# SSM tables: upper half of X left as two unsummed products, small Y levels built for 128 channels at once, seed copies on ScalarE

## The chip, the cores and the metric

The kernel runs on one core of one Trainium2 chip. The metric is device time in microseconds (us); lower is better. All traces shown here are of one execution on core 0. One run of the kernel before took 769 us against 607 for the others; such slow runs are left out of every comparison. "Fast" below means the undisturbed state.

## The reference, cut to what matters

Four layers: an SSM convolution, local attention, the same SSM convolution again, local attention again. Only the first SSM layer is touched. It builds, for each of 512 channels, a convolution kernel K of length 2048 from 128 complex modes, and applies it by FFT.

```python
def _A_ref(u, A_re, A_im, B_re, B_im, C_re, C_im, log_dt, Dskip):
    dt = jnp.exp(log_dt)[:, None]
    logdA = dt * (A_re + 1j * A_im)
    dB = dt * (B_re + 1j * B_im)
    P = jnp.exp(logdA[:, :, None] * l[None, None, :])      # 512 x 128 x 2048 powers
    K = jnp.einsum("dn,dnl,dn->dl", Cc, P, dB).real        # one kernel per channel
    ...                                                    # rfft of K and u, product, irfft
    return y + u * Dskip
```

## The kernel before

The 2048 powers are not computed one by one. A time step is split into a pair (e, i): X holds 32 powers, Y holds 64 scaled powers, and K[e, i] is the sum over the 128 modes of X[e] times Y[i], with real and imaginary parts. That sum is a matmul per channel, so TensorE does it, while VectorE has to build X and Y. The 512 channels come in eight "halves" of 64; two halves are one block of 128 channels, for which the FFT work is done.

Tables grow by doubling: a level of m entries becomes 2m entries by two products and one sum (a complex multiplication; `MA` and `MB` hold the multipliers, with the signs folded in). The top of Y is different: there the two products are kept apart in `Y` and `Y2` and *not* added, and TensorE adds them by accumulating one more matmul.

```python
    def double(self, T, m, lev, hc):
        for e0 in range(0, m, HALF):                 # HALF = 8: at most 1024 elements an operation
            ...
            nc.vector.tensor_tensor(v(ta), src, self.mult(self.MA, lev, hc, mm), ALU.mult)
            nc.vector.tensor_tensor(v(tb), src, self.mult(self.MB, lev, hc, mm), ALU.mult)
            nc.vector.tensor_tensor(T[... m + e0:m + e0 + mm ...], ta[...], tb[:, ::-1 ...], ALU.add)

    def x_part(self, X, hc):
        ...
        nc.vector.tensor_copy(X[:, :, :, 1, :]..., self.nu[:, hc]...)
        for lev in range(1, 5):
            self.double(X, 1 << lev, 6 + lev, hc)    # lev 4: 16 -> 32 entries, six operations

    def y_base(self, Y, hc):
        self.nc.vector.tensor_copy(Y[:, :, :, 0, :]..., self.cb[:, hc]...)
        for lev in range(4):
            self.double(Y, 1 << lev, lev, hc)

    def contract(self, X, Y, Y2, hc, half=None):
        ...
        for ds in range(n):                          # 16 channels of each column group
            for m in range(4):                       # real/imaginary, Y or Y2
                for g in range(4):                   # four groups of 32 columns of the array
                    ...
                    if m % 2 == 0:
                        nc.tensor.matmul(psk[32 * g:32 * g + 32, ds, :], xs, Y[...], ...)
                    else:
                        nc.tensor.matmul(psk[32 * g:32 * g + 32, ds, EYB:], xs, Y2[...], ...)
```

That is 256 matmuls per half, each preceded by its weight load: 512 TensorE instructions. The order of the work, cut:

```python
        xcs[0] = cv.u_fft(0)                         # FFT of the input, one block ahead
        for dc in range(4):
            Kt = half(dc * 2, (lambda: k_fft(dc - 1)) if dc > 0 else None)
            if dc > 0:
                cv.finish(dc - 1, xcs.pop(dc - 1), Kt, Xr)    # products pa, pb on VectorE, inverse FFT
            if dc < 3:
                def mid(dc=dc):
                    xcs[dc + 1] = cv.u_fft(dc + 1)
                half(dc * 2 + 1, mid)
        ...                                          # half 7 (of 0..7) in two parts, last block, layer 2
```

`half` builds the tables and then calls `contract` with high priority in the compiler's list scheduler. The tiles `Y`, `Y2` are single-buffered, `X` double.

## Time and profile before

| | kernel before |
|---|---|
| time (median of fast runs) | 607 us |
| span of the profiled run, granted TensorE clock | 606.0 us, 0.888 |
| first contraction starts | 61.7 us |
| last contraction ends | 226.9 us |
| from there to the end | 379.1 us |

The page of the whole run says that VectorE (DVE) is busy most, but a share over the whole span mixes stages:

```profile
span 606.0 us, 12631 instructions
PE 422.6 (70%) x5362; PEld 261.7 (43%) x5402; DVE 497.0 (82%) x942; ACT 323.0 (53%) x449; POOL 12.9 (2%) x50
```

The windows view of just the contraction loop decides it. The columns are the stretch, its length, the busy time and number of instructions of PE (matmul), PEld (weight load), DVE, ACT (ScalarE) and POOL, then the TensorE clock, the DMA share and GB/s:

```profile
core 0: us, PE busy (x) PEld busy (x) DVE busy (x) ACT busy (x) POOL busy (x), PEclk, DMA share, GB/s
61.67:226.90 165.23, 109.12 (x2653) 74.60 (x2664) 154.37 (x290) 79.15 (x94) 1.75 (x12) 0.81 0.48 95
```

VectorE works 154 of 165 us there: it bounds the loop.

Next, the VectorE timeline (start, length, engine, line, operation, output and input tiles, shapes). Table building begins at 38.9 us; the last three rows are part of the last doubling of X:

```profile
38.89 0.27 DVE L476 TENSOR_TENSOR ta<-Ytab,MA 128x128 bf16<-128x128 bf16 x1
...
55.30 1.23 DVE L513 TENSOR_TENSOR Ytab<-Ytab,MA 128x2048 bf16<-128x2048 bf16 x1
...
59.50 0.69 DVE L476 TENSOR_TENSOR ta<-Xtab,MA 128x1024 bf16<-128x1024 bf16 x1
60.11 0.68 DVE L477 TENSOR_TENSOR tb<-Xtab,MB 128x1024 bf16<-128x1024 bf16 x1
60.83 0.69 DVE L478 TENSOR_TENSOR Xtab<-ta,tb 128x1024 bf16<-128x1024 bf16 x1
```

The TensorE timeline of the first contraction shows matmuls in groups of four, and then a hole. The bracket gives the idle time and what ended it; "issue" means that the profile shows nothing the engine waited for:

```profile
61.67 0.25 PE L532 MATMUL psk<-Ytab,Xtab 128*32 128x64 bf16 x4 [3.00 <-DVE Xtab L478]
...
63.74 0.23 PE L535 MATMUL psk<-Y2tab,Xtab 128*32 128x48 bf16 x1
65.75 0.20 PE L535 MATMUL psk<-Y2tab,Xtab 128*32 128x48 bf16 x3 [1.78 <-issue]
```

From 61.67 to 63.74 us some 180 matmuls ran, about 12 ns each. Then came 1.78 us of nothing. Each contraction before, but for the last, which is split in two, has at least one such hole; from start to end one takes 4.7 to 10.6 us.

On ScalarE one group, the normalization of the input, ends at 61.1 us. And on TensorE, the last contraction is followed at once by the FFT of the last channels:

```profile
50.39 10.67 ACT L575 ACTIVATE X<-X,ln_nb_a,ln_rstd_a 128x512 bf16<-128x512 bf16 x15
```

```profile
226.64 0.22 PE L535 MATMUL psk<-Y2tab,Xtab 128*32 128x48 bf16 x4
226.79 0.20 PE L204 MATMUL psA<-KT,sb_F 128*128 128x64 bf16 x1
```

### The profile page before, as it was taken

How to read it: one execution, taken by the hardware profiler on the slowest of the kernel's cores; microseconds unless marked ns; L12 is line 12 of the kernel's file. 1: busy time of each engine (PE TensorE's matmuls, PEld its weight loads, DVE VectorE, ACT ScalarE, POOL GpSimd, SP SyncE). 2: the span in 40 equal slices, each digit the busy share in tenths (PEclk: the TensorE clock that was granted, in tenths of full speed). 3: DMA queues.
4: the chain of work that ended last, by engine and by line, in shares of the span. 5: the costliest groups of instructions: out<-in, count | busy, mean ns of one | idle time of the engine just before them, and what ended most of it. 6: DMA issues, size and time to landing. Idle time of an engine off the chain costs nothing.

```text
span 606.0 us, 12631 instructions
## 1 busy us (share of the span) xinstructions
PE 422.6 (70%) x5362; PEld 261.7 (43%) x5402; DVE 497.0 (82%) x942; ACT 323.0 (53%) x449; POOL 12.9 (2%) x50
## 2 busy tenths in 40 slices
PE   1102565865775575559998678977996899857996
PEld 0101343562462463245333466644764433326762
DVE  5999999799899996366877899965999688689950
ACT  4999355455465343526576213466984556722144
POOL 0000000000000002100000000000000000000000
PEclk9999787696797797758999599997998899978999
DMA  8101354624735627510001333005530000040011
GB/s 293 62 1 35 61 104 66 140 55 106 121 98 99 103 91 136 129 70 1 1 1 39 83 137 143 2 1 125 85 71 0 2 1 1 1 121 1 1 71 69
DMA packets 75093, 41.31 MB, mean 68 GB/s; under 512 B 65825, under 2 KB 70818, under 8 KB 73758
## 3 DMA queue, kind: packets, MB, share of 16 engines
q1 hardware_dynamic: 73454, 40.12, 27.2%
q8 instruction: 42, 0.69, 0.5%
q10 hardware_dynamic: 1584, 0.39, 0.3%
q14 instruction: 13, 0.11, 0.1%
HBM read 15.89 MB, written 8.39 MB: 40 GB/s over the span
## 4 chain that ended last, share of the span: by engine, by line
PE 27%; DVE 21%; ACT 9%; issue 7%; DMA 2%; POOL 0%; SPq 0%; POOLq 0%; ACTq 0%
PE ps_qk L822 7%; DVE prod L924 6%; PE ps_o L948 4%; PE ps_v L836 3%; PE Lp L868 2%; PE pt_x L802 2%; PE po L939 2%; DVE prod L863 1%; DVE ln_st_b L152 1%; ACT xc L711 1%; DVE pa L719 1%; DMA zt<-Z 1%; DVE pb L720 1%; ACT oT L942 1%; PE ps_o L950 1%
## 5 line engine op out<-in xcount | busy, mean ns | idle before, releaser
L939 PE MATMUL po<-sb_ident,prod 128*128 128x128 bf16 x1024 | 70.4, 227 | 13.7 <-DVE prod L924 10.3
L939 PEld LDWEIGHTS <-prod 128*128 128x128 bf16 x1024 | 62.3, 102 | 23.5 <-DVE prod L924 20.1
L822 PE MATMUL ps_qk<-xnT,wqk 128*128 128x512 bf16 x245 | 63.7, 391 | 4.3 <-ACT xnT L807 2.3
L855 DVE TENSOR_TENSOR prod<-qT,kT 128x2048 bf16<-128x2048 bf16 (+3 forms) x48 | 43.2, 953 | 14.0 <-ACT qT L824 7.2
L924 DVE TENSOR_TENSOR prod<-V,L 128x2048 bf16<-128x2048 bf16 (+3 forms) x48 | 43.8, 955 | 6.4 <-PE po L939 6.4
L942 ACT CAST oT<-po 128x1024 bf16<-128x1024 f32 x16 | 15.4, 1015 | 56.6 <-PE po L939 56.6
L863 DVE TENSOR_TENSOR prod<-qT,kT 128x2048 bf16<-128x2048 bf16 (+3 forms) x40 | 35.0, 903 | 6.9 <-ACT kT L824 4.3
L204 PE MATMUL psA<-X,sb_F 128*128 128x128 bf16 x128 | 13.7, 237 | 34.5 <-ACT X L575 33.7
L822 PEld LDWEIGHTS <-wqk 128*128 128x128 bf16 x256 | 23.4, 100 | 32.1 <-issue 11.8
L948 PE MATMUL ps_o<-wo_t,oT 128*128 128x512 bf16 x121 | 33.5, 380 | 4.9 <-ACT oT L942 3.9
L204 PEld LDWEIGHTS <-sb_F 128*128 128x128 bf16 x256 | 17.4, 106 | 42.6 <-issue 40.0
L924 DVE TENSOR_TENSOR prod<-Vp,L 128x2048 bf16<-128x2048 bf16 (+3 forms) x40 | 35.0, 903 | 0.0
L532 PE MATMUL psk<-Ytab,Xtab 128*32 128x64 bf16 x1024 | 23.7, 206 | 12.9 <-DVE Ytab L513 5.6
L191 ACT CAST Z<-psA 128x1024 bf16<-128x1024 f32 (+1 forms) x32 | 28.6, 979 | 7.3 <-PE psA L204 7.3
L535 PE MATMUL psk<-Y2tab,Xtab 128*32 128x48 bf16 x1024 | 22.8, 202 | 13.5 <-issue 12.2
L868 PE MATMUL Lp<-prod,sb_bones 128*32 128x512 bf16 x256 | 24.9, 410 | 10.1 <-DVE prod L863 5.1
L513 DVE TENSOR_TENSOR Ytab<-Ytab,MA 128x2048 bf16<-128x2048 bf16 (+1 forms) x33 | 30.7, 931 | 0.2
L152 DVE BATCH_NORM_STATS2 ln_st_b<-X 128x6 f32<-128x384 bf16 (+2 forms) x80 | 23.7, 358 | 8.6 <-ACT X L309 8.6
L515 DVE TENSOR_TENSOR Y2tab<-Ytab,MB 128x2048 bf16<-128x2048 bf16 (+1 forms) x33 | 30.7, 930 | 0.0
L836 PE MATMUL ps_v<-wv,xnT 128*128 128x512 bf16 x126 | 28.2, 379 | 1.8 <-ACT V L838 1.7
L532 PEld LDWEIGHTS <-Xtab 128*32 128x32 bf16 x1024 | 20.9, 105 | 17.8 <-issue 15.5
L222 PE MATMUL psA<-zt,sb_C 128*128 128x512 bf16 x30 | 15.6, 548 | 18.6 <-DMA zt<-Z 14.4
(184 smaller groups left out, 1022.3 us busy)
## 6 DMA issues: line engine op xcount, KB each, us to landing
kt_scratch<-Kt SPq DMA_DIRECT2D x4, 1024.0 KB, 3.9
Kt<-kt_scratch SPq DMA_DIRECT2D x4, 1024.0 KB, 6.8
Vp<-V SPq DMA_DIRECT2D x2, 1568.0 KB, 9.1
X<-in_A_u_dram SPq DMA_DIRECT2D x4, 512.0 KB, 5.1
Xr<-in_A_u_dram SPq DMA_DIRECT2D x4, 512.0 KB, 5.1
out_dram<-X SPq DMA_DIRECT2D x4, 512.0 KB, 2.6
k_scratch<-KTq SPq DMA_DIRECT2D x7, 256.0 KB, 2.0
KT<-k_scratch SPq DMA_DIRECT2D x7, 256.0 KB, 2.8
```

The lines of the kernel that those rows point to most:

```text
L204: nc.tensor.matmul(o, F1[:, j, r, :], rhs_j(j), start=True, stop=not dk)
L513: nc.vector.tensor_tensor(v(Y[:, :, :, q * EYB:(q + 1) * EYB, :]), src, vm(self.mult(self.MA, lev, hc, EYB)), ALU.mult)
L515: nc.vector.tensor_tensor(v(Y2[:, :, :, (q - 1) * EYB:q * EYB, :]), src, vm(self.mult(self.MB, lev, hc, EYB)), ALU.mult)
L532: nc.tensor.matmul(psk[32 * g:32 * g + 32, ds, :], xs, Y[:, m // 2, h, :, t], start=(m == 0), stop=False, skip_group_check=True)
L822: nc.tensor.matmul(ps[:], wqk[:, ct, f0:f0 + 128], xnT[:, ct, s0:s0 + 512], start=(ct == 0), stop=(ct == 3))
L836: nc.tensor.matmul(ps[:].rearrange("p a b -> p (a b)"), xnT[:, ct, j * 128:(j + 1) * 128], wv[:, ct, :], start=(ct == 0), stop=(ct == 3))
L855: nc.vector.tensor_tensor(pr[:, :, (ja - j0) * 128:(ja - j0) * 128 + n], qT[fp][:, :, ja * 128: ja * 128 + n], kT[fp][:, :, (ja - sh) * 12 ...
L863: nc.vector.tensor_tensor(pr[:, :, 0:n], qT[fp][:, :, q0: q0 + n], kT[fp][:, :, k0: k0 + n], ALU.mult)
L868: nc.tensor.matmul(Lp[r0:r0 + 32, w // 4, :], bones[:, w % 4, :], pr[:, f2, hb * 512:(hb + 1) * 512], start=(w % 4 == 0), stop=(w % 4 == 3 ...
L924: nc.vector.tensor_tensor(p2[:, ja - j0: ja - j0 + n, :].rearrange("p j (t d h) -> p (j t) d h", t=2, d=DH), src.rearrange("p j (t d h) -> ...
L939: nc.tensor.matmul(po[f2][:, jj, :], p2[:, jj, f2 * 128:(f2 + 1) * 128], ident[:], start=(w == 0 and jj % 4 == 0), stop=(w == W - 1), skip ...
L948: nc.tensor.matmul(ps[:], oT[:, ft, j * 128:(j + 1) * 128], wo_t[:, ft, :], start=(ft == 0), stop=False)
```

## The change

The intent is to take work off VectorE, which bounds the loop: (a) the last doubling of X becomes two products of 2048 elements, left unsummed, as was already done for Y; TensorE adds them with twice as many matmuls; (b) the small levels of Y are built for both halves of a block at once; (c) the three small copies that seed the tables move to ScalarE. To make room in memory, (d) the FFT of the input is done one step later with one buffer instead of two. The two halves of X now lie in swapped order, so (e) the results are fetched in two pieces that swap them back. Core of the diff, cuts marked with "...":

```diff
-        xc = self.one.tile([128, 4, 2, 512], BF, name="xc", tag="xc", bufs=2)
+        xc = self.one.tile([128, 4, 2, 512], BF, name="xc", tag="xc", bufs=1)
...
+    def y_seed(self, dc):
+        S = self.ty.tile([128, 2, 2, HD, HALF, 2], BF, name="Yseed", tag="Yseed")
+        self.nc.scalar.copy(S[:, :, :, :, 0, :]..., self.cb[:, dc * 2:dc * 2 + 2]...)
+        for lev in range(3):
+            m = 1 << lev
+            self.double(S[:, :, :, :, 0:m, :], S[:, :, :, :, m:2 * m, :], m, lev, dc * 2, dc * 2 + 2)
+        return S
+    def y_base(self, S, hc):
+        Y = self.ty.tile([128, 2, HD, EY, 2], BF, name="Ytab", tag="Ytab")
+        b = hc % 2
+        self.nc.scalar.copy(Y[:, :, :, 0:HALF, :]..., S[:, b]...)
+        self.double(S[:, b:b + 1], Y[:, :, :, HALF:2 * HALF, :].unsqueeze(1), HALF, 3, hc, hc + 1)
+        return Y
...
+    def x_products(self, X, hc):
+        X2 = self.ty.tile([128, 2, HD, EXB, 2], BF, name="X2tab", tag="X2tab")
+        src = X[:, :, :, EX - EXB:EX, :]...
+        for dst, M in ((X[:, :, :, 0:EXB, :], self.MA), (X2[:], self.MB)):
+            nc.vector.tensor_tensor(dst..., src, self.mult(M, 10, hc, hc + 1, EXB), ALU.mult)
+        return X2
...
-            for m in range(4):
+            for m in range(8):
+                c, low, summed = m // 4, m // 2 % 2, m % 2
                 for g in range(4):
...
+                    xs = X2[:, 1 - c, h, :, t] if low else X[:, c, h, :, t]
...
-        xcs[0] = cv.u_fft(0)
...
-                    xcs[dc + 1] = cv.u_fft(dc + 1)
+                    xcs[dc] = cv.u_fft(dc)
...
+        xcs[3] = cv.u_fft(3)
```

More of the change, by code (lines that the diff above doesn't have):

```diff
@@ L31 @@
 EX = 32
+EXB = 16
 EYB = 16
@@ L361, in tmp @@
     def tmp(name):
-        return pp.tile([128, 4, NM], F32, name=name, tag="ktmp", bufs=8)
+        return pp.tile([128, 4, NM], F32, name=name, tag="ktmp", bufs=6)
     tb = tmp("tb")
@@ L368, in ladder @@
     rnd = tmp("rnd")
-    ws = tmp("ws")
+    ws = rnd
     nc.vector.tensor_scalar(rnd[:], tb[:], MAGIC, MAGIC, ALU.add, ALU.subtract)
@@ L375, in ladder @@
     nc.scalar.activation(sn[:], ws[:], ACT.Sin, scale=TWO_PI)
-    cs = tmp("cs")
+    cs = sh
     nc.vector.tensor_tensor(cs[:], sh[:], sh[:], ALU.mult)
@@ L459, in __init__, with mult, double @@
         self.wk = es.enter_context(tc.tile_pool(name="t_w", bufs=1))
-    def mult(self, M, lev, hc, n):
-        return (M[:, lev, hc].rearrange("n c (h t) -> n (c h) t", t=2).unsqueeze(2)
-                .to_broadcast([128, 2 * HD, n, 2]))
-    def double(self, T, m, lev, hc):
+    def mult(self, M, lev, h0, h1, n):
+        return (M[:, lev, h0:h1].rearrange("n b c (h t) -> n (b c h) t", t=2).unsqueeze(2)
+                .to_broadcast([128, (h1 - h0) * 2 * HD, n, 2]))
+    def double(self, src, dst, m, lev, h0, h1):
@@ L467, in double @@
         nc = self.nc
-        for e0 in range(0, m, HALF):
-            mm = min(m, HALF)
-            ta = self.wk.tile([128, 2, HD, HALF * 2], BF, name="ta", tag="ta")
-            tb = self.wk.tile([128, 2, HD, HALF * 2], BF, name="tb", tag="tb")
-            def v(t):
-                return t[:].rearrange("n c h (e t) -> n (c h) e t", t=2)[:, :, 0:mm, :]
-            src = T[:, :, :, e0:e0 + mm, :].rearrange("n c h e t -> n (c h) e t")
-            nc.vector.tensor_tensor(v(ta), src, self.mult(self.MA, lev, hc, mm), ALU.mult)
-            nc.vector.tensor_tensor(v(tb), src, self.mult(self.MB, lev, hc, mm), ALU.mult)
-            nc.vector.tensor_tensor(T[:, :, :, m + e0:m + e0 + mm, :].rearrange("n c h e t -> n c h (e t)"),
-                                    ta[:, :, :, 0:mm * 2], tb[:, ::-1, :, 0:mm * 2], ALU.add)
@@ L481, in build @@
-    def build(self, hc):
+        nb = h1 - h0
+        n = nb * 2 * HD * m * 2
+        ta = self.wk.tile([128, 2 * HD * HALF * 2], BF, name="ta", tag="ta")
+        tb = self.wk.tile([128, 2 * HD * HALF * 2], BF, name="tb", tag="tb")
+        for t, M in ((ta, self.MA), (tb, self.MB)):
+            nc.vector.tensor_tensor(t[:, 0:n].rearrange("n (x e t) -> n x e t", e=m, t=2),
+                                    src.rearrange("n b c h e t -> n (b c h) e t"), self.mult(M, lev, h0, h1, m),
+                                    ALU.mult)
@@ new lines, in v @@
+        def v(t):
+            return t[:, 0:n].rearrange("n (b c h x) -> n b c h x", b=nb, c=2, h=HD)
+        for b in range(nb):
+            nc.vector.tensor_tensor(dst[:, b].rearrange("n c h e t -> n c h (e t)"), v(ta)[:, b], v(tb)[:, b, ::-1],
+                                    ALU.add)
+    def y_seed(self, dc):
+        S = self.ty.tile([128, 2, 2, HD, HALF, 2], BF, name="Yseed", tag="Yseed")
+        self.nc.scalar.copy(S[:, :, :, :, 0, :].rearrange("n b c h t -> n (b c h) t"),
+                            self.cb[:, dc * 2:dc * 2 + 2].rearrange("n b c (h t) -> n (b c h) t", t=2))
+        for lev in range(3):
+            m = 1 << lev
+            self.double(S[:, :, :, :, 0:m, :], S[:, :, :, :, m:2 * m, :], m, lev, dc * 2, dc * 2 + 2)
+        return S
@@ L482, in build, with x_base @@
+    def y_base(self, S, hc):
+        Y = self.ty.tile([128, 2, HD, EY, 2], BF, name="Ytab", tag="Ytab")
+        b = hc % 2
+        self.nc.scalar.copy(Y[:, :, :, 0:HALF, :].rearrange("n c h e t -> n (c h) (e t)"),
+                            S[:, b].rearrange("n c h e t -> n (c h) (e t)"))
+        self.double(S[:, b:b + 1], Y[:, :, :, HALF:2 * HALF, :].unsqueeze(1), HALF, 3, hc, hc + 1)
+        return Y
+    def x_base(self, hc):
         nc = self.nc
-        Y = self.ty.tile([128, 2, HD, EY, 2], BF, name="Ytab", tag="Ytab")
@@ L484, in build @@
-        Y2 = self.ty.tile([128, 2, HD, EY - EYB, 2], BF, name="Y2tab", tag="Y2tab")
         X = self.tx.tile([128, 2, HD, EX, 2], BF, name="Xtab", tag="Xtab")
-        return X, Y, Y2
-    def x_part(self, X, hc):
-        nc = self.nc
-        nc.gpsimd.memset(X[:, 0, :, 0, :], 1.0)
-        nc.gpsimd.memset(X[:, 1, :, 0, :], 0.0)
-        nc.vector.tensor_copy(X[:, :, :, 1, :].rearrange("n c h t -> n (c h) t"),
-                              self.nu[:, hc].rearrange("n c (h t) -> n (c h) t", t=2))
-        for lev in range(1, 5):
-            self.double(X, 1 << lev, 6 + lev, hc)
@@ L497, in y_base @@
-    def y_base(self, Y, hc):
-        self.nc.vector.tensor_copy(Y[:, :, :, 0, :].rearrange("n c h t -> n (c h) t"),
-                                   self.cb[:, hc].rearrange("n c (h t) -> n (c h) t", t=2))
-        for lev in range(4):
-            self.double(Y, 1 << lev, lev, hc)
-    def y_products(self, Y, Y2, hc, h0=0, h1=HD):
+        B = X[:, :, :, EX - EXB:EX, :]
+        nc.gpsimd.memset(B[:, 0, :, 0, :], 1.0)
+        nc.gpsimd.memset(B[:, 1, :, 0, :], 0.0)
+        nc.scalar.copy(B[:, :, :, 1, :].rearrange("n c h t -> n (c h) t"),
+                       self.nu[:, hc].rearrange("n c (h t) -> n (c h) t", t=2))
@@ new lines, in x_base @@
+        B = B.unsqueeze(1)
+        for lev in range(1, 4):
+            m = 1 << lev
+            self.double(B[:, :, :, :, 0:m, :], B[:, :, :, :, m:2 * m, :], m, 6 + lev, hc, hc + 1)
+        return X
+    def x_products(self, X, hc):
+        nc = self.nc
+        X2 = self.ty.tile([128, 2, HD, EXB, 2], BF, name="X2tab", tag="X2tab")
+        src = X[:, :, :, EX - EXB:EX, :].rearrange("n c h e t -> n (c h) e t")
+        for dst, M in ((X[:, :, :, 0:EXB, :], self.MA), (X2[:], self.MB)):
+            nc.vector.tensor_tensor(dst.rearrange("n c h e t -> n (c h) e t"), src,
+                                    self.mult(M, 10, hc, hc + 1, EXB), ALU.mult)
+        return X2
@@ L505, in y_products @@
+    def y_products(self, Y, hc, h0=0, h1=HD):
         nc = self.nc
+        if h0 == 0:
+            self.Y2 = self.ty.tile([128, 2, HD, EY - EYB, 2], BF, name="Y2tab", tag="Y2tab")
+        Y2 = self.Y2
         if h1 - h0 == HD:
@@ L513, in y_products, with contract @@
                 nc.vector.tensor_tensor(v(Y[:, :, :, q * EYB:(q + 1) * EYB, :]), src,
-                                        vm(self.mult(self.MA, lev, hc, EYB)), ALU.mult)
+                                        vm(self.mult(self.MA, lev, hc, hc + 1, EYB)), ALU.mult)
                 nc.vector.tensor_tensor(v(Y2[:, :, :, (q - 1) * EYB:q * EYB, :]), src,
-                                        vm(self.mult(self.MB, lev, hc, EYB)), ALU.mult)
-    def contract(self, X, Y, Y2, hc, half=None):
+                                        vm(self.mult(self.MB, lev, hc, hc + 1, EYB)), ALU.mult)
+        return Y2
+    def contract(self, X, X2, Y, Y2, hc, half=None):
         nc = self.nc
@@ L529, in contract @@
                     h, t = d // 2, d % 2
-                    xs = X[:, m // 2, h, :, t]
-                    if m % 2 == 0:
-                        nc.tensor.matmul(psk[32 * g:32 * g + 32, ds, :], xs, Y[:, m // 2, h, :, t],
+                    rows = slice(32 * g, 32 * g + (EXB if low else EX))
+                    xs = X2[:, 1 - c, h, :, t] if low else X[:, c, h, :, t]
+                    if not summed:
+                        nc.tensor.matmul(psk[rows, ds, :], xs, Y[:, c, h, :, t],
                                          start=(m == 0), stop=False, skip_group_check=True)
                     else:
-                        nc.tensor.matmul(psk[32 * g:32 * g + 32, ds, EYB:], xs, Y2[:, 1 - m // 2, h, :, t],
-                                         start=False, stop=(m == 3), skip_group_check=True)
+                        nc.tensor.matmul(psk[rows, ds, EYB:], xs, Y2[:, 1 - c, h, :, t],
+                                         start=False, stop=(m == 7), skip_group_check=True)
         if half != 1:
@@ L543, in contract, with fetch @@
                           KTq.rearrange("p (c x) -> p c x", c=4))
-    def fetch(self, KT, hc):
-        self.nc.sync.dma_start(KT[:, hc % 2], self.kscr[hc].rearrange("g p x -> p g x"))
+    def fetch(self, dst, hc, x0=0, x1=256):
+        src = self.kscr[hc][:, :, x0:x1].rearrange("g p x -> p g x")
+        self.nc.sync.dma_start(dst[0:64], src[64:128])
+        self.nc.sync.dma_start(dst[64:128], src[0:64])
 def kernel_and_first_conv(nc, tc, C, prm, x2d, const, kt_dram, kscr, ln, ln_b):
@@ L581, in kernel_and_first_conv @@
         xcs = {}
+        seeds = {}
         def half(hc, between=None):
-            Xt, Y, Y2 = T.build(hc)
             if hc == 0:
-                T.y_base(Y, hc)
-                T.x_part(Xt, hc)
-            else:
-                T.x_part(Xt, hc)
-                T.y_base(Y, hc)
-            T.y_products(Y, Y2, hc)
+                seeds[0] = T.y_seed(0)
+                Y = T.y_base(seeds[0], hc)
+                Xt = T.x_base(hc)
+            else:
+                Xt = T.x_base(hc)
+                if hc % 2 == 0:
+                    seeds[0] = T.y_seed(hc // 2)
+                Y = T.y_base(seeds[0], hc)
+            X2 = T.x_products(Xt, hc)
+            Y2 = T.y_products(Y, hc)
             r = between() if between is not None else None
             with tc.high_priority():
-                T.contract(Xt, Y, Y2, hc)
+                T.contract(Xt, X2, Y, Y2, hc)
             return r
@@ L599, in k_fft @@
             for h in range(h0, h1):
-                T.fetch(KT, dc * 2 + h)
+                T.fetch(KT[:, h].rearrange("p g j d -> p g (j d)"), dc * 2 + h)
             n = (h1 - h0) * 64
@@ L624, in mid @@
                 def mid(dc=dc):
-                    xcs[dc + 1] = cv.u_fft(dc + 1)
+                    xcs[dc] = cv.u_fft(dc)
                 half(dc * 2 + 1, mid)
         Xr = residual(3)
-        Xt, Y, Y2 = T.build(7)
-        T.x_part(Xt, 7)
-        T.y_base(Y, 7)
-        T.y_products(Y, Y2, 7, 0, HD // 2)
-        T.y_products(Y, Y2, 7, HD // 2, HD)
+        xcs[3] = cv.u_fft(3)
+        Xt = T.x_base(7)
+        Y = T.y_base(seeds[0], 7)
+        X2 = T.x_products(Xt, 7)
+        T.y_products(Y, 7, 0, HD // 2)
+        Y2 = T.y_products(Y, 7, HD // 2, HD)
         Kt = k_fft(3, 0, 1)
         with tc.high_priority():
-            T.contract(Xt, Y, Y2, 7, 0)
-            T.contract(Xt, Y, Y2, 7, 1)
+            T.contract(Xt, X2, Y, Y2, 7, 0)
+            T.contract(Xt, X2, Y, Y2, 7, 1)
         xc = xcs.pop(3)
@@ L648, in kernel_and_first_conv @@
             for u in range(2):
-                nc.sync.dma_start(KT[:, u].rearrange("p g j d -> p g (j d)"),
-                                  kscr[7][:, :, u * 128:u * 128 + 128].rearrange("g p x -> p g x"))
+                T.fetch(KT[:, u].rearrange("p g j d -> p g (j d)"), 7, u * 128, u * 128 + 128)
                 cv.spectrum32(KT[:, u], Drow[:, D - 64 + u * 32:D - 32 + u * 32], Kt[:, 2 + u],
```

## The prediction

> **What bounds the kernel now.** Only the first stage changes; from the first attention layer on the compiled order is identical. In the timeline, tables run from 36 us to the last contraction's end, 226.9 us; 379 us follow. Between first and last contraction (61.7 to 226.9 us) the windows view has VectorE busy 154 of 165 us: it is the bound. A half (64 channels) takes 20.2 us, or 27-29 with the convolution's pa/pb.
>
> **Removed and added on VectorE** (durations: groups of instructions). X's last doubling: six 1024-element ops of 0.69 us become two 2048-element ones of 1.22: -1.7 us a half. Small Y levels pairwise: 5.9 to 4.8 us per two halves, -0.6 a half. Two seed copies of 0.23 go to ScalarE. About 2.7 us a half, 21.7 in all, on the bounding engine.
>
> **What it costs elsewhere.**
> 1. *Contraction.* 256 matmuls per half become 512 (with weight loads, 512 to 1024 instructions). They run at some 12 ns each, but in every contraction the timeline has PE "issue" gaps of 1.1 to 2.5 us. In the compiled order all lie multiples of 256 instructions apart; successive crossings are 3.3 to 4.0 us apart. The Trainium skill, "Runtime: NRT & Kernel Launch", section "Instruction fetch mechanics", says instructions come in blocks of 256, the fetch mostly hidden; this trace agrees on the block, not on hidden. Estimate: contraction 5-7 us now, four blocks or 11.7-14 us after. Y, Y2, X2 are single-buffered, so the next half has only 6.5 us (odd) or 11 us (even) of VectorE work before it waits. The loop becomes contraction + 0.7 + 1.1 + 6.8 = 20.5 us at best, no gain.
> 2. *Start.* ScalarE is busy without a gap from 13.5 to 61.1 us, the last 10.7 us normalizing X. The compiled order puts the seed copy that now starts Y behind that, and all Y/X work behind the seed. VectorE, which now builds tables from 38.9 us, will idle from 48 to 61 us; then 19 us of work: first contraction at 80 instead of 61.7 us.
> 3. *Tail.* In the compiled PE order, part of u_fft(2), and all of k_fft(2), finish(2) and u_fft(3), now stand after the last contraction; before, only the last channels' work did. From their copies in the trace (first FFT stage 3.8, transposing DMA 4.4, second stage 7, inverse 7, final 4; forward 14; rest 4) this is about +44 us in series.
> 4. pa/pb and one ScalarE Ytab copy stand behind k_fft in two halves: periods of 30 and 35 us.
>
> Walking the engines by hand: contractions start near 80, 101, 121, 152, 172, 208, 230, 248 us, the last ends near 260 (+33), tail +44: 607 + 77 gives about 682 us.
>
> **Prediction:** 682 us, 8 in 10 within 650 to 708. Faster by over 2%: 0.02; within 2%: 0.03; slower: 0.95.
>
> **What would show it.** Timeline: VectorE gap before the first Yseed op, ending on ScalarE at 61 us; first contraction at 80. Three PE issue gaps of about 2.3 us in each contraction. VectorE waits before the level-3 Ytab add, released by PE psk, 4-6 us in odd halves. VectorE busy in total down about 22 us. About 85 us from the last contraction to attention's first transposes rather than 41. Later stages unchanged within 2 us.
>
> **What would make it wrong.** Fetch reaching further ahead (-20 us); a warm PE clock in the tail (-10 us); fetch slowed by transposes sharing the DMA engines (+15 us).

## More of the kernel before

The waits view of VectorE before 230 us (who is waited for, us in total, times, longest) confirms that it almost never waits for TensorE to release a table:

```profile
DVE Ytab L498 <- PE psk L535: 3.5, 2, 2.7
```

## The result, and the profile after

The changed kernel takes 700.7 us (median of 4 fast runs, 697.0 to 702.0) against 607.2 before, ratio 1.155, 95% interval 1.1505 to 1.1596: slower. Ratios here are made from fast runs alone; they are not quite the ratio of the medians quoted. The prediction, 682 us in 650 to 708, held the result; its three parts can now be checked separately.

| stage (us) | before | after | difference |
|---|---|---|---|
| start of the span to the first contraction matmul | 61.7 | 79.7 | +18.1 |
| first matmul to the end of the last contraction | 165.2 | 198.0 | +32.8 |
| from there to the first FFT matmul of the last channels | 0 | 43.7 | +43.7 |
| from there to the end | 379.2 | 378.8 | -0.4 |
| span | 606.0 | 700.2 | +94.2 |

VectorE's busy time fell, as intended, and so did its share. The bounding engine now waits:

```profile
span 700.2 us, 16727 instructions
PE 469.4 (67%) x7410; PEld 297.6 (43%) x7450; DVE 479.3 (68%) x870; ACT 334.5 (48%) x469; POOL 12.6 (2%) x50
```

**The start.** In the VectorE timeline there is a hole of 14 us before the first table operation, and it is ScalarE that ends it:

```profile
61.38 0.39 DVE L475 TENSOR_TENSOR ta<-Yseed,MA 128x256 bf16<-128x256 bf16 x1 [14.16 <-ACT Yseed L488]
```

The ScalarE timeline shows why. The seed copy of 0.41 us stands in the queue behind the long normalization, which is unchanged from before:

```profile
50.37 10.66 ACT L609 ACTIVATE X<-X,ln_nb_a,ln_rstd_a 128x512 bf16<-128x512 bf16 x15
60.94 0.41 ACT L488 COPY Yseed<-cb 128x256 bf16<-128x256 bf16 x1
```

**The loop.** The first contraction now has three holes instead of one. Between each two "issue" rows lie exactly 128 matmuls, that is, 256 instructions; from one hole's end to the next it takes 3.5 and 4.0 us, although the matmuls in between need only about 1.5:

```profile
79.73 0.24 PE L563 MATMUL psk<-Ytab,Xtab 128*32 128x64 bf16 x4 [3.90 <-DVE Xtab L524]
...
84.30 0.22 PE L566 MATMUL psk<-Y2tab,X2tab 128*16 128x48 bf16 x4 [1.62 <-issue]
...
87.76 0.22 PE L566 MATMUL psk<-Y2tab,X2tab 128*16 128x48 bf16 x4 [1.78 <-issue]
...
91.76 0.22 PE L566 MATMUL psk<-Y2tab,X2tab 128*16 128x48 bf16 x4 [2.33 <-issue]
```

So a contraction takes 13 to 14 us when it runs alone. The next half may write `Y` only when it is over. VectorE has some other work to fill the time, then it stands; the waits view (before 280 us) and two rows of its timeline:

```profile
DVE Ytab L482 <- PE psk L566: 41.4, 6, 13.2
DVE ta L475 <- ACT Yseed L488: 14.2, 1, 14.2
```

```profile
93.11 0.69 DVE L482 TENSOR_TENSOR Ytab<-ta,tb 128x1024 bf16<-128x1024 bf16 x1 [5.89 <-PE psk L566]
142.26 0.69 DVE L482 TENSOR_TENSOR Ytab<-ta,tb 128x1024 bf16<-128x1024 bf16 x1 [13.23 <-PE psk L566]
```

Against 3.5 us before, VectorE now waits 41 us for contractions. The windows view of the first period, the third, and the stretch after the last contraction shows VectorE idle for part of each, most of all in the third and in the last (busy 20.4 of 39.1 us and 12.6 of 43.7). The columns are those of the windows view before:

```profile
80.30:101.00 20.70, 6.83 (x508) 6.09 (x509) 14.60 (x21) 2.48 (x4) 0.24 (x2) 0.50 0.09 29
...
121.50:160.60 39.10, 30.49 (x622) 19.59 (x623) 20.40 (x31) 13.89 (x18) 0.23 (x2) 0.59 0.30 69
277.70:321.40 43.70, 29.43 (x209) 17.77 (x210) 12.57 (x24) 24.07 (x29) 0.00 (x0) 0.78 0.41 94
```

The wait of 13.2 us belongs to the third contraction, which took 20.7 us. In its middle, TensorE alternated between one full-array matmul of the FFT (128*128, of line 205) and one narrow matmul of the contraction (128*32 or 128*16), at 0.37 us a pair, from 131.2 to 140.7 us:

```profile
133.06 0.29 PE L205 MATMUL psA<-KT,sb_F 128*128 128x128 bf16 x1
133.28 0.22 PE L563 MATMUL psk<-Ytab,X2tab 128*16 128x64 bf16 x1
133.44 0.29 PE L205 MATMUL psA<-KT,sb_F 128*128 128x128 bf16 x1
```

**The tail.** Before, the FFT of the last channels followed the last contraction at once. Now the rest of the input FFT of block 2, the kernel FFT, products, inverse and final stage of block 2 and the input FFT of block 3 come first, and the last channels' FFT starts 43.7 us later:

```profile
277.67 0.61 PE L223 MATMUL psA<-zt,sb_C 128*128 128x512 bf16 x1
...
321.38 0.19 PE L205 MATMUL psA<-KT,sb_F 128*128 128x64 bf16 x1
```

### The profile page after: what moved, and what is told of

It is laid out like the page before. It is cut to its first block, busy times and chain, and to the rows that moved or that the text cites. A ratio compares the mean times of both kernels' runs of the same rounds, so it can differ in the third digit from the quotient of the medians.

```text
span 700.2 us, 16727 instructions
## 1 busy us (share of the span) xinstructions
PE 469.4 (67%) x7410; PEld 297.6 (43%) x7450; DVE 479.3 (68%) x870; ACT 334.5 (48%) x469; POOL 12.6 (2%) x50
## 4 chain that ended last, share of the span: by engine, by line
PE 23%; DVE 16%; ACT 7%; issue 6%; DMA 2%; SPq 1%; POOL 0%; another core or an unknown queue 0%; POOLq 0%; ACTq 0%; DVEq 0%
PE ps_qk L859 6%; DVE prod L961 5%; PE ps_o L985 3%; PE ps_v L873 3%; PE Lp L905 2%; PE po L976 1%; PE pt_x L839 1%; DVE ln_st_b L153 1%; DVE prod L900 1%; DVE pa L756 1%; ACT xc L748 1%; DVE pb L757 1%; DMA zt<-Z 1%; ACT oT L979 1%; PE ps_o L987 1%
## 5 line engine op out<-in xcount | busy, mean ns | idle before, releaser
L976 PE MATMUL po<-sb_ident,prod 128*128 128x128 bf16 x1024 | 72.7, 232 | 11.4 <-DVE prod L961 7.9
L976 PEld LDWEIGHTS <-prod 128*128 128x128 bf16 x1024 | 65.2, 105 | 20.6 <-DVE prod L961 17.2
L563 PE MATMUL psk<-Ytab,Xtab 128*32 128x64 bf16 x1024 | 49.0, 220 | 33.0 <-DVE Ytab L541 16.5
L563 PE MATMUL psk<-Ytab,X2tab 128*16 128x64 bf16 x1024 | 49.8, 218 | 22.0 <-issue 21.2
L566 PE MATMUL psk<-Y2tab,Xtab 128*32 128x48 bf16 x1024 | 47.6, 218 | 9.3 <-issue 6.7
L566 PE MATMUL psk<-Y2tab,X2tab 128*16 128x48 bf16 x1024 | 48.1, 217 | 7.8 <-issue 7.8
L563 PEld LDWEIGHTS <-Xtab 128*32 128x32 bf16 x1024 | 38.5, 119 | 33.3 <-issue 32.5
L563 PEld LDWEIGHTS <-X2tab 128*16 128x16 bf16 x1024 | 36.1, 108 | 19.1 <-issue 16.8
L566 PEld LDWEIGHTS <-Xtab 128*32 128x32 bf16 x1024 | 36.5, 110 | 15.4 <-issue 14.4
L267 DVE TENSOR_TENSOR pa<-xc,Kt 128x1024 bf16<-128x1024 bf16 x16 | 11.0, 690 | 42.4 <-ACT Kt L192 33.0
L566 PEld LDWEIGHTS <-X2tab 128*16 128x16 bf16 x1024 | 33.0, 98 | 15.4 <-issue 14.2
L510 ACT COPY Xtab<-nu 128x128 bf16<-128x128 bf16 x8 | 2.4, 311 | 71.7 <-issue 55.0
```

The source lines that it names most:

```text
L563: nc.tensor.matmul(psk[rows, ds, :], xs, Y[:, c, h, :, t], start=(m == 0), stop=False, skip_group_check=True)
L566: nc.tensor.matmul(psk[rows, ds, EYB:], xs, Y2[:, 1 - c, h, :, t], start=False, stop=(m == 7), skip_group_check=True)
L976: nc.tensor.matmul(po[f2][:, jj, :], p2[:, jj, f2 * 128:(f2 + 1) * 128], ident[:], start=(w == 0 and jj % 4 == 0), stop=(w == W - 1), skip ...
```

## The experiments

The theory after the result: the change has three separate costs. (1) The start costs about 15 to 18 us because the first seed waits for ScalarE. (2) Twice the contraction instructions cost time in instruction fetch, not in matmul work, and make VectorE wait. (3) The later input FFT lengthens the tail. The rivals: for (2), that the narrow matmuls themselves or their half-rate clock are slow; and in general, that undoing one part gains nothing, because another limit lies right behind.

Each run was timed beside the kernel before on the same chip. Where only a profile was taken, the state of the single run is unknown and only the trace is used.

### Seeds of the first half back on VectorE

```diff
-        self.nc.scalar.copy(S[:, :, :, :, 0, :]...
+        (self.nc.vector.tensor_copy if dc == 0 else self.nc.scalar.copy)(S[:, :, :, :, 0, :]...
```

(The same for the copies into `Ytab` and `Xtab` of half 0.)

> The changed kernel, with only the three small copies of the first half (Yseed from cb, Ytab from Yseed, Xtab from nu) put back on VectorE. Theory (ScalarE order): VectorE no longer waits 14.2 us for ScalarE at 61 us; the first contraction starts near 62 instead of 80 us and everything after it moves forward as it is: 700.7 - 18 = 682 us (678 to 687), contractions still 12 to 20 us, last contraction to the next first FFT stage still about 44 us. Rival (the late start costs little, because later waits would have absorbed it): within 4 us of 700.7.

Measured: 685.9 us (685.0 to 688.4), ratio to before 1.132 [1.1266, 1.1374], against 1.155 for the full change: some 15 us came back. The first contraction starts at 60.5 us instead of 79.7, so of the 19 us gained at the start about 4 are lost again in the loop: VectorE's wait for contractions rose from 41.4 to 48.2 us. Cost (1) is shown.

### X summed again, half the contraction matmuls

```diff
+        nc.vector.tensor_tensor(X[:, :, :, 0:EXB, :], X[:, :, :, 0:EXB, :], X2[:, ::-1], ALU.add)
-            for m in range(8):
-                c, low, summed = m // 4, m // 2 % 2, m % 2
+            for m in range(4):
+                c, low, summed = m // 2, 0, m % 2
```

One more VectorE operation of 1.2 us per half, and everything else as in the changed kernel.

> The changed kernel, with the upper half of X summed after all by one more VectorE addition of 2048 elements a half, so that a contraction has 256 matmuls again; start and order of the FFTs left as changed. Theory (instruction blocks of 256 limit the contraction, and the single-buffered tables hand this to VectorE): contractions 5 to 7.5 us, VectorE's waits for psk fall from 45 us to under 10, first contraction still near 80, its last near 237 instead of 278, some 32 us of FFT work still after it: about 648 us (640 to 656). Rival (the waits come from somewhere else, for example the lower TensorE clock or the copies on ScalarE): above 685 us.

Measured: 638.1 us (636.7 to 640.7), ratio 1.0537 [1.0475, 1.06]. So some 62 us came back for an operation added to the engine that was to be relieved. Contractions take 5.2 to 6.4 us, and VectorE's wait for them is gone. The loop (82.3 to 222.7 us) took 140.4 us, less than the 165.2 before, with VectorE busy 135.1 us of it. The other parts of the change do save VectorE work, but less than these numbers suggest: over the whole run its busy time fell by 10.2 us (497.0 to 486.8). The rest is mostly work that moved: the products `pa` and `pb` of block 2 (5.5 us) now stand after the last contraction. The tail is 412.6 us from there, 33 more than before.

The unsummed products are the largest cost.

### The kernel before, with the input FFT one step later

```diff
-        xc = self.one.tile([128, 4, 2, 512], BF, name="xc", tag="xc", bufs=2)
+        xc = self.one.tile([128, 4, 2, 512], BF, name="xc", tag="xc", bufs=1)
-        xcs[0] = cv.u_fft(0)
-                    xcs[dc + 1] = cv.u_fft(dc + 1)
+                    xcs[dc] = cv.u_fft(dc)
+        xcs[3] = cv.u_fft(3)
```

> The kernel before, with only the forward FFT of each channel block moved one step later and its result single-buffered, as in the change. Theory (the tail is serial): the forward FFT of the last block stands after the last contraction, 3.1 (first stage) + 4.7 (transposing DMA) + 6.1 us (second stage) = +14 us: 621 us (617 to 626); everything up to the last contraction within 3 us of before. Rival (it is hidden behind other waits of the tail): under 610 us.

Measured: 618.0 us (616.9 to 619.0), ratio 1.0192 [1.0146, 1.0239]; whether that passes 2% is not settled, that it is slower is. The last contraction ends at 225.5 us, about as before, and the tail is 391.7 us, 12.6 more. Moving the FFT alone costs some 12 us, all of it after the last contraction. The 43.7 us of the changed kernel's tail are thus not the move alone: there, the kernel FFT, the products and the inverse of block 2 also stand behind the last contraction.

### Shorter matmuls, same number of instructions

```diff
-                        nc.tensor.matmul(psk[rows, ds, :], xs, Y[:, c, h, :, t], ...
+                        w = EY if m == 0 else 16
+                        nc.tensor.matmul(psk[rows, ds, 0:w], xs, Y[:, c, h, 0:w, t], ...
-                        nc.tensor.matmul(psk[rows, ds, EYB:], xs, Y2[:, 1 - c, h, :, t], ...
+                        nc.tensor.matmul(psk[rows, ds, EYB:32], xs, Y2[:, 1 - c, h, 0:16, t], ...
```

Seven of eight matmuls stream 16 columns instead of 64 or 48. This leaves out terms of the sum, so it is no kernel to keep (the comparison with the reference still passed).

> The changed kernel, with seven of the eight matmuls of each channel streaming 16 columns instead of 64 or 48 (wrong results on purpose). The number of instructions is the same. Theory (instruction fetch): the contractions stay at 12 to 14 us where nothing is interleaved, with gaps after the same number of matmuls and 3.3 to 4.0 us from one gap's end to the next; total within 1% of the changed kernel. Rival (streaming in the array at a low clock sets the length): gap to gap falls by 1 us or more, contractions under 9 us, total at least 15 us less.

Measured: 699.9 us, a single run, and a first contraction of 12.9 us against 13.4. The timeline of that contraction:

```profile
83.96 0.19 PE L567 MATMUL psk<-Y2tab,X2tab 128*16 128x16 bf16 x4 [2.03 <-issue]
...
87.69 0.19 PE L567 MATMUL psk<-Y2tab,X2tab 128*16 128x16 bf16 x4 [2.51 <-issue]
...
91.42 0.19 PE L567 MATMUL psk<-Y2tab,X2tab 128*16 128x16 bf16 x4 [2.51 <-issue]
```

The holes became longer by what the matmuls became shorter; from hole to hole it is 3.73 us, both times. The contraction is bound by the number of instructions, not by what they compute. Nor is it the TensorE clock: from hole to hole it took 3.45 us at a granted clock of 0.50 (the changed kernel at 84.30 us) and 3.45 us at 0.96 (the run with full-array matmuls below, at 183.17 us).

### 32 matmuls more before the first contraction

```diff
+        if hc == 0:
+            for _ in range(32):
+                nc.tensor.matmul(psk[0:32, 0, :], X[:, 0, 0, :, 0], Y[:, 0, 0, :, 0], start=True, stop=True, ...)
```

> The changed kernel with 32 more matmuls (64 instructions with their weight loads) in front of the first contraction, whose results are overwritten. Theory (a stall at each block of 256 instructions): in every contraction the gaps come after 32 matmuls fewer: in the first contraction, counting its own matmuls, near 124, 252, 380 instead of 156, 284, 412, in the second near 123 instead of 155. Rival (gaps at fixed places of the program, or at fixed times): counts as in the changed kernel. Total within 1% of it.

Measured: 701.7 us, a single run. The three holes come after 124, 252 and 380 matmuls of the contraction; in the changed kernel they come after 156, 284 and 412. They moved by exactly 32 matmuls, so they sit at fixed places of the instruction stream, 256 instructions apart, and not at any channel or table. The first hole is short here (the added matmuls all use one column group and run slowly, 30 of them in 1.76 us, which covers most of it):

```profile
83.08 0.21 PE L570 MATMUL psk<-Y2tab,X2tab 128*16 128x48 bf16 x4 [0.26 <-issue]
...
87.08 0.20 PE L570 MATMUL psk<-Y2tab,X2tab 128*16 128x48 bf16 x4 [2.33 <-issue]
...
90.53 0.22 PE L570 MATMUL psk<-Y2tab,X2tab 128*16 128x48 bf16 x4 [2.25 <-issue]
```

Together with the run before, this shows cost (2): from one hole to the next, a block of 256 TensorE instructions takes 3.5 to 4.0 us here, whatever is in it.

What ends the holes stands in the traces too, though not in the brackets. The page of each run lists the DMA queues (packets, MB, share of 16 engines), and one is of the kind "instruction". The first row is of the kernel before, the second of the changed one:

```profile
q8 instruction: 42, 0.69, 0.5%
q8 instruction: 58, 0.95, 0.6%
```

A packet of this queue holds 16,384 bytes, and 16 more packets go with 4096 more TensorE instructions: one packet for 256 of them. The DMA view of the changed kernel from 81 to 92 us, in its first contraction, shows nothing else:

```profile
DMA packets 3, 0.05 MB, mean 4 GB/s; under 512 B 0, under 2 KB 0, under 8 KB 0
q8 instruction: 3, 0.05, 2.0%
```

By their records these three ran from 81.94 to 83.05, 85.45 to 86.40 and 88.80 to 90.20 us, and the three holes ended at 84.30, 87.76 and 91.76 us, each 1.3 to 1.6 us after a packet. The next packet starts 1.0 to 1.2 us after a hole's end, so here the fetch is only one block ahead. In the 14 traces of this case together, 179 holes inside contractions (over 0.9 us from matmul to matmul, without a releaser) all end 1.2 to 1.6 us after such a packet. So the holes are the fetch of instructions. The Trainium skill, "Runtime: NRT & Kernel Launch", section "Instruction fetch mechanics", describes a refill in blocks of 256 instructions; these traces agree.

### The unsummed products alone

The kernel before, with the later input FFT of the third run, plus the unsummed X; the small levels of Y per half and all copies on VectorE, as before (against the changed kernel):

```diff
-        self.nc.scalar.copy(Y[:, :, :, 0:HALF, :]..., S[:, b]...)
-        self.double(S[:, b:b + 1], Y[...].unsqueeze(1), HALF, 3, hc, hc + 1)
+        self.nc.vector.tensor_copy(Y[:, :, :, 0, :]..., self.cb[:, hc]...)
+        for lev in range(4):
+            m = 1 << lev
+            self.double(Y1[:, :, :, :, 0:m, :], Y1[:, :, :, :, m:2 * m, :], m, lev, hc, hc + 1)
```

> The kernel before with the later forward FFT of e3 and with the upper half of X left as two products; no Y levels for 128 channels, no copies on ScalarE. Compared with e3 (618 us) it shows the cost of the unsummed products alone. Theory: contractions 12 to 14 us, VectorE can do only about 5.5 us of the next half meanwhile, halves of 25 to 26 us instead of 20: 665 us (655 to 680), although VectorE has 13 us less to do. Rival (VectorE remains the limit): 605 to 615 us.

Measured: 711.7 us (710.2 to 712.3), ratio 1.172 [1.1696, 1.1744]. The expectation was missed by 47 us. Against the third run (618.0 us, on another chip but with the same time of the kernel before within 0.3%), which differs in the unsummed X and the fetch in two pieces, the products cost 94 us, not the 47 that I had expected. The trace says where: the contraction that starts at 119.3 us ends at 172.4. The scheduler had placed 16 matmuls of the second FFT stage and 64 of the inverse between its own matmuls, one by one, at about 0.70 and 0.49 us a pair:

```profile
133.78 0.61 PE L224 MATMUL psA<-zt,sb_C 128*128 128x512 bf16 x1
134.32 0.22 PE L565 MATMUL psk<-Ytab,X2tab 128*16 128x64 bf16 x1
134.47 0.61 PE L225 MATMUL psA<-zt,sb_C 128*128 128x512 bf16 x1
```

The same pattern, in milder form, is the 20.7 us contraction of the changed kernel. The lesson is that a long contraction not only waits for its instructions; it also stays open long enough for other work to become ready and be woven into it. But is it the weaving that costs, or the extra work alone? The run with added matmuls below asks that.

### Both repairs: first seeds on VectorE, X summed

The edits of the first two runs together, against the changed kernel:

```diff
+        (self.nc.vector.tensor_copy if dc == 0 else self.nc.scalar.copy)(S[:, :, :, :, 0, :]...   # and two more
+        nc.vector.tensor_tensor(X[:, :, :, 0:EXB, :], X[:, :, :, 0:EXB, :], X2[:, ::-1], ALU.add)
+            for m in range(4):
```

> Both repairs in the changed kernel: first three copies on VectorE, upper half of X summed. Theory (the two costs add): first contraction near 62, last one over near 205, 33 us of FFT work still after it: 638 - 16 = 622 us (616 to 627). If the start had been hidden by the FFT work of the TensorE queue: 630 to 638.

Measured: 619.1 us (617.5 to 622.3), ratio 1.0205 [1.017, 1.024]. Here the surprise is what was not gained. The last contraction ends at 203.6 us, 23 us earlier than in the kernel before, with VectorE busy 135 of 141 us in the loop. But the tail is 412 us against 379: all of it is gone, and the result is some 2% slower. Not all of the 23 us was a gain, though. After the last contraction stand the products of two blocks here (8 `pa` and 8 `pb`), in the kernel before those of one, and VectorE's busy time over the whole run fell by only 10.5 us (497.0 to 486.5). Even these 10.5 us do not show in the time: with the later input FFT alone it was 618.0 us.

### Only the light parts, on the kernel before

The small copies go to ScalarE from the second half on, and the last doubling of X is done as two products and one sum of 2048 elements. Unsummed products, pairs and the later FFT stay out.

```diff
-        nc.vector.tensor_copy(X[:, :, :, 1, :]...
+        (nc.vector.tensor_copy if hc == 0 else nc.scalar.copy)(X[:, :, :, 1, :]...
-        for lev in range(1, 5):
+        for lev in range(1, 4):
             self.double(X, 1 << lev, 6 + lev, hc)
+        tab = self.wk.tile([128, 2, HD, 16, 2], BF, name="tab", tag="tab")
+        nc.vector.tensor_tensor(tab..., src, self.mult(self.MB, 10, hc, 16), ALU.mult)
+        nc.vector.tensor_tensor(top..., src, self.mult(self.MA, 10, hc, 16), ALU.mult)
+        nc.vector.tensor_tensor(top..., top..., tab[:, ::-1]..., ALU.add)
```

(And the copy into `Y` likewise.)

> A version that should beat both: the kernel before (order of the FFTs, 256 matmuls), with the small copies on ScalarE from the second half on, and X's last doubling as two products of 2048 and one addition of 2048 instead of six operations of 1024. VectorE has about 0.45 us (copies) and 0.6 us (doubling) less a half: -8 us: 598 us (593 to 603). If VectorE's saving is taken back by waits for TensorE or ScalarE: 603 to 608.

Measured: 607.8 us (607.0 to 608.7), ratio 1.0017 [0.9993, 1.0041]: the same. VectorE's busy time in the loop (61.6 to 228.2 us here) fell from 154.4 to 150.6 us, but it now waits 6.4 us for copies by ScalarE:

```profile
DVE tab L476 <- ACT Ytab L505: 3.3, 1, 3.3
DVE tab L476 <- ACT Xtab L492: 3.1, 1, 3.1
```

The rival ("taken back") held. Two copies of 0.2 to 0.3 us came back as waits of 3 us each, on an engine whose queue holds evacuations of 1 us.

### Full-array matmuls between narrow ones

To measure the weaving by itself, 30 dummy full-array matmuls (weights: the identity) were added to two contractions of the kernel before: in the fourth half, one before every eight contraction matmuls; in the sixth, all 30 ahead as a block.

```diff
+        for i in range(30 if hc == 5 else 0):
+            full(i)
         for ds in range(n):
             for m in range(4):
+                if hc == 3 and m % 2 == 0 and ds < 15:
+                    full(ds * 2 + m // 2)
```

> The kernel before with 30 dummy matmuls that use the whole array (128x128 weights, 48 columns, results overwritten) in two of its contractions: in the fourth half one before every eight of the contraction's matmuls (which use 32 columns of the array each), in the sixth all 30 ahead of the contraction. Same instructions in both. Theory (matmuls that use the whole array and matmuls that use a quarter of its columns can't overlap, so alternating costs about 0.3 to 0.45 us a pair, as seen where FFT stages stand between contraction matmuls): the fourth half's contraction takes 10 us or more, start to end, the sixth's with its dummies 6 to 9 us. Rival (only the added instructions count): both the same within 1.5 us.

Measured: 621.0 us, a single run, and the result was wrong (relative error 0.039). The dummies were meant to be overwritten; why they left a trace was not followed up, so only the timing of the instructions is used. The woven contraction lasts 11.0 us (130.7 to 141.7), the one with the block ahead 7.5 us (179.5 to 186.9). The first rows are of the woven one, the last of the block:

```profile
138.56 0.22 PE L526 MATMUL psk<-Y2tab,sb_ident 128*128 128x48 bf16 x1
138.92 0.22 PE L526 MATMUL psk<-Y2tab,sb_ident 128*128 128x48 bf16 x1
...
179.45 0.91 PE L526 MATMUL psk<-Y2tab,sb_ident 128*128 128x48 bf16 x30 [0.46 <-DVE Y2tab L515]
```

A round of one full and eight narrow matmuls takes 0.29 us in the first four rounds, where the granted clock was 1.00, and 0.37 us in the others, where it was 0.50. The block ran at 0.96: there a full matmul takes 0.03 us and eight narrow ones 0.06, in sum 0.09 us. So at nearly the same clock a round costs 0.2 us more when woven (an estimate from these numbers), for two changes between the full array and its column groups. The comparison of the two whole contractions, 11.0 against 7.5 us, holds the fall of the clock too, and is no measure of the changes alone. The Trainium skill, "TensorEngine Tiling (Array Packing)", section "Tiling Modes", says under "Key Properties" that "Changing tiling mode (not just tile) drains the TensorE"; this run agrees as far as it shows a cost of the change (the drain itself is not visible), and puts a number to it. That in turn explains most of the 7.3 us by which the 20.7 us exceed the first contraction: 26 such changes and back at 0.37 us took 9.6 us, in place of the 2.6 us that 26 FFT matmuls need at the 0.10 us from start to start that five of them in a row took at 122.15 us, at the same half clock.

### Towards a kernel that beats both

The repairs of the seventh run, plus the input FFT early again with two buffers, and, to make room, one buffer for the FFT intermediate Z instead of two:

```diff
-        xc = self.one.tile([128, 4, 2, 512], BF, name="xc", tag="xc", bufs=1)
+        xc = self.one.tile([128, 4, 2, 512], BF, name="xc", tag="xc", bufs=2)
-        cv = Conv(nc, tc, es, C, X, psA, ())
+        cv = Conv(nc, tc, es, C, X, psA, (), zbufs=1)
+        xcs[0] = cv.u_fft(0)
-                    xcs[dc] = cv.u_fft(dc)
+                    xcs[dc + 1] = cv.u_fft(dc + 1)
-        xcs[3] = cv.u_fft(3)
```

> All three costs taken out of the change: first copies on VectorE, upper half of X summed (256 matmuls), forward FFT one step early again with double-buffered results; to make room, the FFT's Z has one buffer. VectorE keeps most of the saving. Theory (costs add): first contraction near 62, last one over near 205, after it only the last block's usual work and one inverse (about 19 us) that the compiled TensorE order still puts there: 603 us (594 to 609), against 607 before. If the single Z buffer stalls the FFTs: above 609.

Measured: 612.6 us (611.4 to 615.5), ratio 1.0099 [1.0047, 1.015], above the 609 us that had been set as the sign of stalls on the single Z; no run shows that the single Z is the cause. The last contraction ends at 213.3 us, where 205 had been expected, and the tail is 398.5. VectorE waits 14.3 us for the transformed kernels, the longest time 11 us, all of it after the last contraction; before that it waits 5.4 us for copies of Y by ScalarE.

A further step gave the last kernel FFT high priority in the scheduler:

```diff
-        Kt = k_fft(3, 0, 1)
+        with tc.high_priority():
+            Kt = k_fft(3, 0, 1)
```

> As e10, with the kernel spectrum's FFT of the last block ahead of the inverse of the block before it in the TensorE queue, so that its DMA latencies overlap that inverse. 4 to 8 us less than e10: 597 us (588 to 604).

Measured: 611.9 us (609.4 to 614.9), ratio 1.0085 [1.0039, 1.0132]. It did not help measurably. The expectation (597 us) fell.

Finally the large X operations alone on the kernel before, without the copies on ScalarE (the small copies stay on VectorE):

```diff
-        for lev in range(1, 5):
+        for lev in range(1, 4):
             self.double(X, 1 << lev, 6 + lev, hc)
+        nc.vector.tensor_tensor(tab..., src, self.mult(self.MB, 10, hc, 16), ALU.mult)
+        nc.vector.tensor_tensor(top..., src, self.mult(self.MA, 10, hc, 16), ALU.mult)
+        nc.vector.tensor_tensor(top..., top..., tab[:, ::-1]..., ALU.add)
```

> The kernel before with the last doubling of X as two products and one addition of 2048 elements in place of six operations of 1024, and nothing else: the small copies stay on VectorE. From the groups' means that is 6 x 0.69 = 4.1 us against 3 x 1.22 = 3.7 us, some 0.5 us a half or 4 us in all on VectorE, which is busy 154 of 165 us in the loop. Theory (the loop is bound by VectorE as long as no new wait is made; in the run with both light parts the waits for ScalarE's copies, 6.4 us, ate the gain): 603 us, 601 to 606, and VectorE's busy time in the loop some 4 us shorter, no waits for ScalarE copies. Rival (TensorE's chain of FFT work is the second limit right behind, so a faster VectorE in the loop is given back in the waits for Kt or after the last contraction): same as before within 0.3%, with the last contraction ending earlier or waits for Kt longer.

Measured: 604.9 us (603.4 to 606.0) against 605.5 for the kernel before in the same rounds, ratio 0.9965 [0.9922, 1.0008]: the same within what can be told. In the trace the loop takes 163.3 us (60.9 to 224.2) instead of 165.2, with VectorE busy 151.8 us and no wait for ScalarE copies. So about half of the 4 us hoped for shows in the loop, and theory and rival are not told apart by the time. It is the best of the versions tried, and no proven gain.

## Why the prediction was right or wrong

The prediction's direction and its range held; its median, 682, was 18.7 us low. Point by point:

- *"VectorE is the bound."* Right for the loop before (154 of 165 us). The run with both repairs adds something the prediction did not have: the 10.5 us that VectorE saved there did not show in the time. That the FFT chain behind the loop, through TensorE, transposing DMAs and ScalarE, is the reason is likely, but no run tests it.
- *Removed VectorE work, 21.7 us.* VectorE's total busy time fell by 17.7 us (497.0 to 479.3). A part of the difference is that durations were added up while neighbouring operations overlap: by durations, one operation of 2048 elements in place of two of 1024 saves 0.16 us (two times 0.69 less 1.22), by start to start 0.08 us (two times 0.61 less 1.14). The Trainium skill, "Vector Engine (DVE) Microarchitecture Reference", section "5.2 Measured stream behaviour on trn2", gives about 75 ns per instruction "after queue overlap" (for 32-bit data; here it is bf16); this trace agrees: 1.14 less 0.61 is 0.53 us for 1024 elements, which leaves 0.08 us per operation.
- *Start, first contraction at 80 us.* Right: 79.7, with a gap of 14.2 us ended by ScalarE's seed copy at 61.4 us. The first run shows the cause.
- *Contraction bound by instruction blocks, three holes in each, 11.7 to 14 us, the loop +33 us less the start.* The mechanism was right, the size too small. Holes after 156, 284 and 412 matmuls, moving with the instruction stream and not shrinking with the matmuls, were shown by two runs. Five of the eight contractions took 13.1 to 14.7 us, in the upper part of the range or just beyond.
- *"Walking the engines by hand: ... 80, 101, 121, 152, 172, 208, 230, 248 us, the last ends near 260."* This is the step that failed. Measured: 80, 101, 122, 161, 184, 216, 244, 263, end 277.7. The first three agree within 1 us. Of the 17.7 us at the end, 8 arise in the third period alone, whose contraction took 20.7 us: the hand walk charged nothing for the kernel FFT's matmuls being woven into the contraction, and they ran at 0.37 us a pair. The traces also tell of the other two long ones, though no run varied them. The fourth took 16.1 us; near its end seven FFT matmuls are woven in (174.0 to 176.6 us), again at 0.37 us a pair. The sixth took 18.4 us: 23 FFT matmuls stand in a row behind its first four (215.7 to 219.0 us), and then comes a hole of 4.4 us, because the instruction packet starts only at 222.37 us, when the last packet of a 1 MB write to `kt_scratch` (219.14 to 222.36 us) is through. In the trace of the first run the packet also starts as this write ends (207.6 us), and that hole has 4.2 us. That weaving can cost this much was shown by the added matmuls, and, by accident, by the unsummed products alone.
- *Tail, +44 us.* Right: 43.7. But the third run shows that of this only some 12 us come from moving the FFT alone. With X summed again the tail is still 33 us longer than before, so most of the rest does not come from the unsummed products; which other part makes it, no run separates.
- *Later stages unchanged within 2 us.* Right: 378.8 against 379.2 us.
- *VectorE waits 4 to 6 us in odd halves* (counted from 0). Right in kind, too small: 5.9, 13.2, 6.0 and 7.2 us in halves 1, 3, 5 and 7, and 1.1, 3.1 and 7.9 us in halves 2, 4 and 6, where none was expected.
- *What would make it wrong.* Of the three named reasons, only the third, a fetch slowed by other DMA traffic, shows clearly: in the one hole of 4.4 us, behind a write and not behind transposes, some 2 us more than the usual hole (an estimate).

## What to carry to other kernels

Before moving work from a bound engine to TensorE as more and smaller matmuls, count instructions, not columns: in this kernel 256 TensorE instructions (128 matmuls with their weight loads) took 3.5 to 4.6 us from hole to hole in all runs, whatever they computed, so doubling 512 to 1024 cost some 7 us per half to save under 2 us of VectorE, and the longer run invited full-array matmuls into it, at some 0.2 us for each change and back (the estimate above). A small copy is cheap only where the queue that it joins is empty. When a bound engine has been relieved, look at what stands after the loop before counting the gain.

## What the Trainium skill lacked or had wrong

- "Runtime: NRT & Kernel Launch", section "Instruction fetch mechanics", says that crossing a block boundary is mostly hidden and that the fetch is hidden behind the issue of instructions. For short matmuls it is not: holes of mostly 1.1 to 2.8 us (up to 4.4 behind a large write) every 256 TensorE instructions, 3.5 to 4.6 us from hole to hole in contractions, in the kernel before as in all the others; with matmuls of 16 columns still 3.73 us. Each ends 1.2 to 1.6 us after a packet of the instruction queue.
- The same section gives TensorE room for 2048 instructions. Here the first hole came after 156 matmuls, 312 instructions, of the first contraction although TensorE had been idle for 3.9 us just before; in no run did it come after more than 362 instructions of the first contraction. The packet of the next block started 1.0 to 1.2 us after a hole's end, so the fetch was one block of 256 ahead; how large the memory is, no run shows.
- "TensorEngine Tiling (Array Packing)", section "Tiling Modes", states that a change of mode drains TensorE, without a cost. Runs: at full clock 0.29 us per round of one full-array and eight column-tiled matmuls, where the parts alone need 0.09 us; at half clock 0.37 us per pair with FFT matmuls of 128 columns, against 0.10 from start to start for the FFT matmul in a row of its kind.
